# Where the setup's stores of the first m-tile's later queries are issued: from POOL, ahead of the shift rows, to SP, behind the other chunks' keys

## The chip, the cores and the metric

The kernel runs on one core of a Trainium2 chip. The core has a matrix engine (TensorE, PE in the profile), a vector engine (VectorE, DVE), a scalar engine (ScalarE, ACT), GpSimd (POOL) and a sync engine (SyncE, SP) that here only issues DMA transfers. ACT and POOL issue DMA transfers too. The metric is device time in microseconds (us), the median of several executions. Three runs of the kernel before took 1236.10, 1234.47 and 1240.26 us.

## What is computed

Two layers over the same length of 2048 stand side by side, and their outputs are concatenated. Layer A is a long convolution of a state-space model; layer B is attention with 32 query heads of width 18 that share one key and one value head.

```python
def _B_ref(x, wq, wk, wv, wo):
    q = (x @ wq).reshape(B, S, H, Dh).transpose(0, 2, 1, 3)   # S = 2048, H = 32, Dh = 18
    k = x @ wk
    v = x @ wv
    scores = jnp.einsum("bhqd,bkd->bhqk", q, k) * (Dh ** -0.5)
    p = _softmax(scores, axis=-1)
    o = jnp.einsum("bhqk,bkd->bhqd", p, v)
    return o.transpose(0, 2, 1, 3).reshape(B, S, H * Dh) @ wo
```

Layer A forms a kernel K of length 2048 for each of 576 channels out of complex exponentials, convolves it with the input by an FFT of twice the length, and adds the input times a skip weight. The change lies in layer B; layer A fills the engines beside it.

## The kernel before, in words

**Attention.** The 2048 queries are cut into four chunks of 512 (index c), the 576 query columns into m-tiles of seven heads (index m; the last has four). Scores are computed with the keys on the partitions, 128 keys at a time, and 512 queries of one chunk on the free axis, for two heads (a pair) at once. A product in full precision is made of three parts: the operand is rounded (qh, kh), and what rounding leaves (ql, kl) is multiplied separately. So a head's queries stand as 55 rows in an augmented tile (`aug`): rows 0 to 17 hold qh, 18 to 35 qh again, 36 to 53 ql, and row 54 a shift (sh), an upper bound of the scores, which is subtracted before the exponential. Two heads stand at partitions 0 and 64 of one `aug` tile. The keys stand in `kaug` in the matching rows, with ones in row 54.

**The setup** (lines 209 to 304, function `setup`) loads the input and the weights, projects the keys of all four chunks and the queries of chunk 0's first m-tile, and places the keys: `place(c)` issues six transfers of 18 rows on SP (line 281). `place(0)` serves the first scores. Then the first m-tile's queries are made by a generator that `setup` advances, `first_queries` and, in it, `queries(0, 0, ...)`. For the four heads of the first two pairs, `queries` copies the rows straight into the tiles `aug0` and `aug1` (line 363, on POOL, with qh of the second pair on ACT). The other three heads of the m-tile go to DRAM, into `qd` (line 365): one store of qh to rows 0 to 17, one of qh to rows 18 to 35, one of ql, all on POOL. After the shift has been worked out on PE and DVE (aw, up, un, sh), line 387 writes the shift rows of the first two pairs, on ACT and on SP, and line 389 stores the shift of the other three heads to `qd`, on POOL. Then `setup` issues `place(1)` to `place(3)`, and after them the loads of the other m-tiles' weights (line 207), the transform matrices, the convolution's input and the output weights.

**The main loop** (`main`) runs rounds of three scores, each a pair of heads against 128 keys: six matmuls, three exponentials on ACT, and the products with the values (ops). Between them a planner at build time places all other work, the later m-tiles' projections (q), their bounds (up) and the convolution. It uses modelled costs of PE, ACT and DVE and writes out one fixed order for these three engines. The order of SP and of POOL is chosen by the framework, so there an instruction may stand elsewhere than the program's text says. `fetch` (line 398, on SP) reads the 55 rows of later heads from `qd` into the five `aug` tiles, which are used in turn.

**Names that the change touches.** The tiles qh, ql and sh have one buffer each (`bufs=1`): the copies of the second m-tile's queries (DVE, lines 103 and 99, right after the projection q) write to the same memory that the first m-tile's stores read, and wait for them. All projections and bounds share one PSUM bank (`bank`), which is filled again only after DVE has emptied it. Generators yield what they wait for: "v" for vector work, "p" for matrix work, "w" for nothing in particular; a caller's `advance()` runs one on to its next yield.

Of the kernel before, what the change touches and what calls it, by code (L numbers as in the profile page):

```python
# [9 lines left out]
F32 = mybir.dt.float32  # L10
# [11 lines left out]
DH = 18  # L22
# [141 lines left out]
def matmul4(nc, ps, w, x, start=True, stop=True):  # L164

    n = w.shape[-1]
    for j in range(0, n, 32):
        e = min(n, j + 32)
        nc.tensor.matmul(ps[j:e], w[:, j:e], x, start=start, stop=stop, tile_position=(0, j))  # L169


class Attention:
# [36 lines left out]
    def setup(self, tp, conv):  # L209
# [5 lines left out]
        nc, cp, a, V = self.nc, self.cp, self.a, self.V  # L215
# [62 lines left out]
        def place(c):  # L278
            for r, t in ((0, kh), (36, kh), (18, kl)):
                for b in (0, 64):  # L280
                    nc.sync.dma_start(self.kaug[b + r:b + r + 18, c * CT:(c + 1) * CT].bitcast(F32), t[32 * c:32 * c + 18, :].bitcast(F32))
# [10 lines left out]
            side.advance()  # L292
        for c in range(1, NCH):
            place(c)

        for m in range(2, 5):
            V.memset(self.wq[m][0:1, 0, 0:1], 0.0)
# [50 lines left out]
    def queries(self, c, m, qh, ql, ab):  # L348

        nc, V, K = self.nc, self.V, self.k  # L350
        m0, mn = MT[m]
        h0, h1 = m0 // DH, (m0 + mn) // DH
        if m == 0:
            self.qd[c] = self.dr.tile([H, 55, CT], F32, tag="qd", name=f"qd{c}")
        qd = self.qd[c]

        n0 = 4 if (c, m) == (0, 0) else 0
        for h in range(n0):
            t = self.aug[h // 2]
            for row, src in ((0, qh), (18, qh), (36, ql)):  # L360
                b = 64 * (h % 2) + row
                q = nc.scalar if h // 2 == 1 and row < 36 else nc.gpsimd
                q.dma_start(t[b:b + 18, :].bitcast(F32), src[h * DH:h * DH + DH, :].bitcast(F32))
        for row, src in ((0, qh), (18, qh), (36, ql)):
            nc.gpsimd.dma_start(qd[h0 + n0:h1, row:row + 18, :], src[n0 * DH:mn, :].bitcast(F32))  # L365
        self.first = False
        yield "v", 0.0, False
        aw = self.p2.tile([P, P], F32, tag="aw", name=f"aw{c}_{m}", bufs=1)
        V.tensor_scalar(aw[:mn, :], ab[:mn, 0:1].broadcast_to([mn, P]), self.kmax[:mn, 0:1], None, op0=ALU.mult)
        yield "p", max(K.v + 0.4, K.fill), False  # L370

        up = self.bank(8, f"up{c}_{m}")
        matmul4(nc, up, aw[:mn, :], self.sel[:mn, 0:8])
        K.pe(0.1)
        K.v = max(K.v, K.t + 0.3)
        un = self.p2.tile([P, 1], F32, tag="un", name=f"un{c}_{m}", bufs=4)
        V.tensor_reduce(un, up, axis=AX.X, op=ALU.max)
        K.filled()
        if self.ubound is not None:
            u2 = self.p2.tile([P, 1], F32, tag="u2", name=f"u2_{c}_{m}", bufs=4)  # L380
            V.tensor_tensor(u2, un, self.ubound, op=ALU.max)
            un = u2
        self.ubound = un
        sh = self.p2.tile([8, CT], F32R, tag="sh", name=f"sh{c}_{m}", bufs=1)
        V.tensor_scalar(sh, un[0:8, 0:1].broadcast_to([8, CT]), -1.0, None, op0=ALU.mult)
        for pr in range(n0 // 2):
            (nc.scalar, nc.sync)[pr].dma_start(self.aug[pr][54:119:64, :].bitcast(F32), sh[0:2, :].bitcast(F32))
            self.ready.add(pr)
        nc.gpsimd.dma_start(qd[h0 + n0:h1, 54, :], sh[:h1 - h0 - n0, :].bitcast(F32))
        self.queried = c * H + h1  # L390

    def fetch(self, group):
# [922 lines left out]
```

## Time and profile before

| what | us |
|---|---|
| median of three runs | 1236.10 |
| the profiled execution's own time | 1237.14 |
| its span, from the first to the last instruction | 1235.1 |
| PE busy | 1154.1 |
| ACT busy | 1046.1 |
| DVE busy | 987.2 |
| POOL busy | 57.5 |
| first matmul of the setup | 10.08 |
| last matmul of the setup ends | 31.25 |
| first scores of the main loop | 35.67 |

How to read it: the span is that of one profiled execution; its own time is the span and some 2 us around it, and stands 1.0 us above the median. Times in the views count from the span's start. A line gives the engine, the line of the kernel, the operation and the tiles (out<-in); "q" behind an engine's name (SPq, ACTq) marks its queue of DMA issues and register work, where an entry's length is the issue and not the transfer. A bracket at the end gives the idle time ahead of an instruction and what ended it. The granted clock is the share of TensorE's full clock that the chip allowed.

### The profile page before, as it was taken

How to read it: one execution, taken by the hardware profiler on the slowest of the kernel's cores; microseconds unless marked ns; L12 is line 12 of the kernel's file. 1: busy time of each engine (PE TensorE's matmuls, PEld its weight loads, DVE VectorE, ACT ScalarE, POOL GpSimd, SP SyncE). 2: the span in 40 equal slices, each digit the busy share in tenths (PEclk: the TensorE clock that was granted, in tenths of full speed). 3: DMA queues.
4: the chain of work that ended last, by engine and by line, in shares of the span. 5: the costliest groups of instructions: out<-in, count | busy, mean ns of one | idle time of the engine just before them, and what ended most of it. 6: DMA issues, size and time to landing. Idle time of an engine off the chain costs nothing.

```text
span 1235.1 us, 32531 instructions
## 1 busy us (share of the span) xinstructions
PE 1154.1 (93%) x13762; PEld 473.4 (38%) x13762; DVE 987.2 (80%) x1604; ACT 1046.1 (85%) x1101; POOL 57.5 (5%) x97
## 2 busy tenths in 40 slices
PE   5899999999999999999999899999999999899997
PEld 1344334344344344344334334334433334334333
DVE  4668978986987986896898895797798897897753
ACT  2689979989988888888988888888989988999992
POOL 2110000100100000000000000000010000000000
PEclk9899999999999899999999899999999999999999
DMA  7541221222232012023313002122122212012111
GB/s 219 176 133 53 73 69 60 75 75 78 79 104 83 34 38 81 26 72 103 95 57 120 21 20 77 52 76 71 50 75 79 72 35 77 15 51 86 47 41 41
DMA packets 55402, 89.29 MB, mean 72 GB/s; under 512 B 14620, under 2 KB 25244, under 8 KB 54740
## 3 DMA queue, kind: packets, MB, share of 16 engines
q1 hardware_dynamic: 43972, 72.19, 17.9%
q0 software_dynamic: 10592, 14.39, 4.4%
q8 instruction: 110, 1.80, 0.6%
q10 hardware_dynamic: 688, 0.57, 0.2%
q14 instruction: 40, 0.33, 0.1%
HBM read 49.25 MB, written 36.50 MB: 69 GB/s over the span
## 4 chain that ended last, share of the span: by engine, by line
PE 67%; DVE 20%; ACT 6%; issue 4%; DMA 2%; POOL 0%; SPq 0%; ACTq 0%; DVEq 0%
PE ops L708 27%; PE s L409 19%; ACT P L417 5%; PE op L169 4%; DVE tab L99 4%; PE q L169 4%; PE kg L1028 3%; DVE ks L99 3%; PE iy L169 3%; DVE acc L99 2%; DMA xr<-xT 2%; PE hk L169 2%; DVE f L99 1%; DVE r L99 1%; PE lk L169 1%
## 5 line engine op out<-in xcount | busy, mean ns | idle before, releaser
L417 ACT ACTIVATE P<-s 128x1024 f32<-128x1024 f32 x1024 | 967.7, 1030 | 151.2 <-PE s L409 144.1
L708 PE MATMUL ops<-P,v_sb 128*32 128x512 f32 x4096 | 523.4, 603 | 9.9 <-DVE o L103 9.8
L409 PE MATMUL s<-aug,kaug 55*128 55x512 f32 x2048 | 365.4, 444 | 27.3 <-ACT P L417 21.0
L409 PEld LDWEIGHTS s<-aug,kaug 55*128 55x128 f32 x2048 | 170.2, 186 | 344.0 <-ACT P L417 309.6
L708 PEld LDWEIGHTS ops<-P,v_sb 128*32 128x32 f32 x4096 | 115.9, 110 | 160.0 <-issue 120.5
L169 PE MATMUL q<-x,wq_sb 128*32 128x256 f32 (+2 forms) x1480 | 102.7, 396 | 5.1 <-DVE un L111 2.6
L169 PE MATMUL op<-wo_sb,oT 126*32 126x288 f32 (+1 forms) x1088 | 79.7, 416 | 6.2 <-DVE sck L99 3.7
L169 PEld LDWEIGHTS q<-x,wq_sb 128*32 128x32 f32 (+2 forms) x1480 | 46.9, 110 | 57.4 <-issue 27.5
L103 DVE COPY ksb<-kg 128x192 f32<-128x192 f32 x48 | 17.5, 364 | 56.7 <-PE kg L1028 56.7
L99 DVE TENSOR_TENSOR tab<-tab,tt 128x576 f32<-128x576 f32 (+1 forms) x72 | 59.2, 822 | 1.6
L99 DVE TENSOR_TENSOR tab<-tab 128x576 f32<-128x576 f32 (+1 forms) x72 | 59.0, 820 | 0.9
L99 DVE TENSOR_TENSOR tt<-f,sum 128x576 f32<-128x576 f32 (+1 forms) x72 | 58.9, 818 | 0.0
L99 DVE TENSOR_TENSOR tab<-sum,r 128x576 f32<-128x576 f32 (+1 forms) x72 | 58.9, 818 | 0.0
L99 DVE TENSOR_TENSOR tab<-r,dif 128x576 f32<-128x576 f32 (+1 forms) x72 | 58.8, 816 | 0.0
L169 PEld LDWEIGHTS op<-wo_sb,oT 126*32 126x32 f32 (+1 forms) x1088 | 31.9, 111 | 48.3 <-issue 23.9
L365 POOL DMA_DIRECT2D qd<-qh x40 | 25.3, 637 | 514.4 <-DVE qh L103 514.4
L99 DVE TENSOR_TENSOR acc<-acc,pt 128x1728 f32<-128x1728 f32 (+2 forms) x36 | 48.6, 1351 | 0.1
L99 DVE TENSOR_TENSOR pt<-us,ks 128x1728 f32<-128x1728 f32 (+2 forms) x36 | 48.6, 1351 | 0.0
L99 DVE TENSOR_TENSOR sck<-lk,sck 128x384 f32<-128x384 f32 x48 | 24.5, 552 | 29.7 <-PE lk L169 29.7
L1028 PEld LDWEIGHTS kg<-tab 128*32 128x32 f32 x2304 | 36.0, 110 | 23.2 <-issue 9.2
L1028 PE MATMUL kg<-tab 128*32 128x64 f32 x2304 | 41.8, 220 | 1.3 <-DVE tab L99 1.1
L99 DVE TENSOR_TENSOR ks<-ks 128x576 f32<-128x576 f32 (+1 forms) x48 | 41.0, 854 | 0.9
(123 smaller groups left out, 944.5 us busy)
## 6 DMA issues: line engine op xcount, KB each, us to landing
aug<-qd SPq DMA_DIRECT2D x124, 110.0 KB
od<-o SPq DMA_DIRECT2D x31, 256.0 KB
qd<-qh POOLq DMA_DIRECT2D x30, 252.0 KB, 5.2
u<-u SPq DMA_DIRECT2D x12, 384.0 KB
kd<-ksb SPq DMA_DIRECT2D x12, 384.0 KB
kt<-kd SPq DMA_DIRECT2D x48, 96.0 KB
outa<-u SPq DMA_DIRECT2D x12, 384.0 KB
oT<-od SPq DMA_DIRECT2D x16, 252.0 KB
```

The lines of the kernel that those rows point to most:

```text
L99: return self.v.tensor_tensor(out, *a, **k)
L103: return self.v.tensor_copy(out, *a, **k)
L169: nc.tensor.matmul(ps[j:e], w[:, j:e], x, start=start, stop=stop, tile_position=(0, j))
L365: nc.gpsimd.dma_start(qd[h0 + n0:h1, row:row + 18, :], src[n0 * DH:mn, :].bitcast(F32))
L409: nc.tensor.matmul(ps[:, j, :], self.kaug[r, kb * P:(kb + 1) * P], t[r, :], start=True, stop=True)
L417: nc.scalar.activation(pt, ps, AF.Exp, scale=SCALE)
L708: nc.tensor.matmul(o_ps[32 * j:32 * j + 32, :], self.v[:, kb, :], pts[2 * n + j // 2][:, j % 2, :], start=(kb == 0), stop=(kb == 15), tile ...
L1028: nc.tensor.matmul(ps[32 * g:32 * g + 32, d, :], t[:, :32], t[:, 32:], start=(j == 0), stop=(j == 1), tile_position=(0, 32 * g))
```

## The change

The three stores of line 365 become a function `store(q)`, which takes the engine that issues them. For every m-tile but the first of chunk 0 it is called at the old place with POOL. For the first (where four heads went straight into the `aug` tiles, so `n0` is 4) the generator yields once more after the shift rows, and only then issues the three stores and the shift's store, all on SP. In `setup` one `side.advance()` behind the three `place` calls runs this part. So SP issues four more transfers between the last key rows and the weight loads, and POOL four fewer.

```diff
@@ setup
         for c in range(1, NCH):
             place(c)
+        side.advance()
 
         for m in range(2, 5):
@@ queries
-        for row, src in ((0, qh), (18, qh), (36, ql)):
-            nc.gpsimd.dma_start(qd[h0 + n0:h1, row:row + 18, :], src[n0 * DH:mn, :].bitcast(F32))
+        def store(q):
+            for row, src in ((0, qh), (18, qh), (36, ql)):
+                q.dma_start(qd[h0 + n0:h1, row:row + 18, :], src[n0 * DH:mn, :].bitcast(F32))
+        if n0 == 0:
+            store(nc.gpsimd)
         self.first = False
         yield "v", 0.0, False
@@ queries, behind the shift rows
-        nc.gpsimd.dma_start(qd[h0 + n0:h1, 54, :], sh[:h1 - h0 - n0, :].bitcast(F32))
+        q = nc.gpsimd if n0 == 0 else nc.sync
+        if n0:
+            yield "w", 0.0, False
+            store(q)
+        q.dma_start(qd[h0 + n0:h1, 54, :], sh[:h1 - h0 - n0, :].bitcast(F32))
         self.queried = c * H + h1
```

## The prediction

> **What bounds the kernel now.** I read the page first, for the whole span, and the waits of TensorE next.
>
> ```profile
> span 1235.1 us, 32531 instructions
> PE 1154.1 (93%) x13762; PEld 473.4 (38%) x13762; DVE 987.2 (80%) x1604; ACT 1046.1 (85%) x1101; POOL 57.5 (5%) x97
> PE s L409 <- ACT P L417: 21.0, 62, 0.5
> PE s L409 <- DMA qd<-qh: 4.4, 1, 4.4
> ```
>
> PE is busy 93% of the span. Outside the loads at the start its waits are small and many; only one of 4.4 us stands alone, ahead of the first scores. The build writes out one order for PE, ACT and DVE, so a delay of PE early in the main loop can only be made up where PE has slack later. A table of stretches shows how little there is (columns: length, busy time of PE, PEld, DVE, ACT, POOL with instruction counts, granted clock, DMA share, GB/s).
>
> ```profile
> 31.25:35.67 4.42, 0.00 (x0) 0.03 (x1) 4.25 (x12) 0.00 (x0) 1.11 (x2) 0.85 0.40 97
> 35.67:41.20 5.53, 5.53 (x42) 2.93 (x46) 3.41 (x8) 2.86 (x3) 0.00 (x0) 0.50 0.22 63
> 41.20:48.68 7.48, 7.48 (x83) 3.05 (x75) 3.63 (x7) 6.19 (x7) 1.86 (x3) 1.00 0.42 115
> 48.68:61.00 12.32, 12.32 (x148) 4.95 (x146) 9.42 (x14) 10.89 (x12) 0.55 (x1) 1.00 0.87 290
> 200.00:1190.00 990.00, 942.19 (x11304) 388.29 (x11298) 826.36 (x1322) 876.12 (x921) 35.74 (x57) 0.99 0.20 64
> ```
>
> PE is full from 35.67 to 61 and 95% busy (942.19 of 990) in the long middle. So whatever shift PE has when it comes out of the first 60 us, I carry to the end one for one. The second row matters too: after 4.42 us without a matmul PE works for 5.53 us at a granted clock of 0.50, which costs half of that, 2.8 us.
>
> What holds the first scores? They read the augmented queries and the keys, and nothing of qd, so the name in the wait is not the cause. The timeline of ACT, SP and POOL and the table of DMA issues (last number: us from issue to landing) show what is under way:
>
> ```profile
> 29.84 0.61 ACTq L387 DMA_DIRECT2D aug<-sh  x1
> 30.77 0.57 SPq L387 DMA_DIRECT2D aug<-sh  x1
> 31.38 13.95 SPq L281 DMA_DIRECT2D kaug<-keys  x17
> ...
> 27.93 2.01 POOL L363 DMA_DIRECT2D aug<-ql  x4
> 29.92 1.31 POOL L365 DMA_DIRECT2D qd<-qh  x2
> 31.22 0.61 POOL L365 DMA_DIRECT2D qd<-ql  x1
> 31.82 0.54 POOL L389 DMA_DIRECT2D qd<-sh  x1
> ...
> aug<-ql POOLq DMA_DIRECT2D x4, 36.0 KB, 2.6
> qd<-qh POOLq DMA_DIRECT2D x2, 108.0 KB, 5.9
> qd<-ql POOLq DMA_DIRECT2D x1, 108.0 KB, 5.8
> qd<-sh POOLq DMA_DIRECT2D x1, 6.0 KB, 5.6
> ```
>
> The two shift rows are the last writes that the first scores need. They go out at 29.84 and 30.77, PE starts at 35.67, so they took up to 5.8 and 4.9 us, while the queries' rows just before landed in 2.6. In between stand POOL's stores; even the one of 6 KB needed 5.6. The stores delay the shift rows: this is what the change takes out.
>
> **The change, part by part.** *The shift rows.* Without the stores I give them the 2.6 us of the ql rows: 30.77 + 2.6 = 33.4, so PE would start at about 33.4, 2.3 us earlier (bounds: nothing, and 4.4, all of its idle time). POOL loses four issues, 2.5 us of an engine that is 5% busy: nothing.
>
> *The stores on SP.* They now stand behind seventeen key rows. The rows of line 281:
>
> ```profile
> 32.20 13.13 SPq L281 DMA_DIRECT2D kaug<-keys  x16
> L281 SPq DMA_DIRECT2D kaug<-keys x24: 697/698/2001, 24.8 to 44.6; - x24
> 45.44 0.88 SPq L207 DMA_DIRECT2D wq_sb<-wq  x2
> ```
>
> One of the sixteen took 2.00 us, while POOL's stores ran; the other fifteen take (13.13 - 2.00)/15 = 0.742 each. With all at that pace the keys end at 31.38 + 17 x 0.742 = 44.0 (45.3 if the long one stays). SP's issues of such rows cost 0.74 with the gap, so the stores go out at 44.0, 44.7 (qh), 45.5 (ql), 46.2 (shift row), and the next loads at about 46.9 in place of 45.44.
>
> *A new wait on DVE.* The tiles qh, ql and sh have one buffer each. The second m-tile's queries overwrite qh and ql, so their DVE copies must wait until the stores have read the first ones. Before, the stores had landed by 31.22 + 5.8 = 37.0 and the copy came at 44.94, waiting only for PE. Rows of DVE, then of PE:
>
> ```profile
> 44.94 0.69 DVE L103 CAST qh<-q 126x512 fp32r<-126x512 f32 x1 [5.86 <-PE q L169]
> 45.67 0.69 DVE L99 TENSOR_TENSOR ql<-q,qh 126x512 fp32r<-126x512 f32 x1
> 46.99 0.29 DVE L107 TENSOR_SCALAR aw<-ab,kmax 126x128 f32<-126x128 f32 x1
> 49.33 0.16 DVE L111 TENSOR_REDUCE un<-up 128x1 f32<-128x8 f32 x1
> ...
> 47.55 1.20 PE L409 MATMUL s<-aug,kaug 55*128 55x512 f32 x6
> 48.68 0.25 PE L169 MATMUL up<-sel_sb,aw 126*32 126x8 f32 x8
> 51.49 1.93 PE L169 MATMUL q<-x,wq_sb 128*32 128x256 f32 x32
> ```
>
> No store of this kind runs on SP before. Its landing time is bounded below by the 36 KB rows' 2.6 us and above by the worst store row (8.7 us, below); I take 5.8, the ql store of the same shape. Then qh is free at 44.7 + 5.9 = 50.6 and ql at 45.5 + 5.8 = 51.3. From the start of the ql subtraction to the end of aw DVE needs 47.28 - 45.67 = 1.6, so aw ends at 52.9 and up can run at 53.0, against 48.68: **4.3 us later**. With the bounds 2.6 and 8.7 it is 48.1 + 1.7 = 49.8 (1.1 later) and 54.2 + 1.7 = 55.9 (7.2 later).
>
> Who waits behind: on DVE the table products of the convolution from 47.20 on, then un and sh; on PE, in its fixed order, behind up stand products with the values, the next scores and the third m-tile's projection; ACT gets no scores meanwhile. The 2.3 us won at the start go into this wait: PE, earlier by 2.3, comes to up at about 46.4 and stands there 6.6 us. What DVE owes afterwards is covered: it sits idle 4.31 us before the next qh (row below), and PE's q at 51.49 came 2.0 us after un (49.33 + 0.16) and keeps that distance.
>
> *The clock.* A PE that stands for 6.6 us is the case of the table's first two rows. I charge 2.5 us for the half clock after it (bounds 0, and the 2.8 of the old stage). The half clock that PE has now at 35.67 may go, but that too lies ahead of up and is lost in the wait.
>
> *What moves on SP.* Every later load slips by about 1.5 us, more where stores and loads share the engines.
>
> ```profile
> 62.62 0.69 DVE L103 CAST qh<-q 126x512 fp32r<-126x512 f32 x1 [4.31 <-PE q L169]
> 60.00 5.67 SPq L398 DMA_DIRECT2D aug<-qd  x6
> 70.26 1.36 PE L409 MATMUL s<-aug,kaug 55*128 55x512 f32 x6
> qd<-qh POOLq DMA_DIRECT2D x2, 252.0 KB, 6.2
> qd<-ql POOLq DMA_DIRECT2D x1, 252.0 KB, 8.7
> SPq L1049 <- DMA kd<-ksb: 37.0, 12, 5.1
> ```
>
> The fetch of the next pairs, issued from 60.00 to 65.67, is first read by the eleventh group of scores at 70.26: 4.6 us of cover, and 11 with PE's own shift. It costs nothing; uncovered it would cost PE a microsecond for each one of slip. The second m-tile's stores, some 6 us later on POOL, have until the DVE copy at 62.62 plus the shift, against landings of 6.2 and 8.7 us from 45.93 on: covered as well.
>
> *The sum.* 4.3 + 2.5 = 6.8 us. The profiled execution took 1237.1 us (span 1235.1 and 2.0 around it), 1.0 above the median of the runs; so it would take 1243.9, and the median 1236.1 + 6.8 = **1242.9**.
>
> [...]
>
> **The rivals.** *Stores that queue up behind each other.* If the three serve one after another, the ql store lands like the later one of the second tile: 8.7 us where qh took 6.2 (rows above). Then up comes at 55.9: 7.2 + 2.5 = 9.7, **1245.8**. For it: in that row the last of three is the late one. Against it: POOL's first three landed in 5.9 and 5.8. [...]
>
> *Stores that land fast.* The 384 KB store kd on SP made its reader wait 37.0/12 = 3.1 us on average; with that, ql is free at 48.6, up comes at 50.3, 1.6 late; with 2.6 us it is 1.1. Add 1.7 to 2.5 for a shorter half clock: about **1239.5**. For it: SP is otherwise quiet at 44 us, POOL was not at 30. Against: the shape is POOL's, and 6 KB there took 5.6.
>
> *No new wait, the gain kept.* If the copy of the second qh did not find the stores in its way, or they landed by 44, PE keeps 2.3 us and perhaps 2.8 of the half clock: **1231 to 1234**, not slower. It decides only if ql is free by about 44.7 (PE at up at 46.4 less 1.7), before the ql store is even issued at 45.5; so it needs another order of SP than the one named.
>
> *Late queries for the second group.* If SP's slip exceeds some 11 us, the scores at 70.26 wait for the fetch: at the point where it decides, 1243 and up, **1250** with 7 us past it. Against: 1.5 us of slip in issues, and 330 KB of stores beside loads that run at 290 GB/s, about 1 us.
>
> That SP does not put the stores there at all (its order is not written out by hand) would leave 1236.
>
> **How the numbers follow.** Forecast 47% (own range 1239.8 to 1244.4, from landings of 3.5 to 7 us and 1.7 to 2.8 for the clock); queued stores 20%; fast landing 17%; gain kept 9%; late fetch 4%; no effect 3%. The range 1234.5 to 1249.5 leaves out the larger part of the kept gain below and of the late fetch above, and holds both bounds of the landing time. A measurement of this kernel tells about 0.5%, 6.2 us, from no change: the line is at 1242.3. Of the forecast's 47 some 28 lie above it, with 20 of the queued stores and 4 of the late fetch: slower 0.52. Faster by 6.2 takes more than all that is to be won at the start, 0.03. The rest, 0.45, is within.
>
> **What would show it.** After: the wait for the first scores shrinks from 4.4 to about 2; SP issues stores at 44 to 46; DVE's qh copy, which waited for PE, is released by a DMA at about 50.6, with some 7 us or more of idle time; PE stands before up until about 53, and the granted clock is 0.50 behind it. Were up at 47 or earlier, the new wait is not there and the gain stands; were the clock full behind the wait, 2.5 us come off; were PE's shift at 61 us not the difference at the end, the carrying one for one is wrong.

## The result, and the profile after

| kernel | runs | median us | lowest to highest |
|---|---|---|---|
| before | 6 | 1238.85 | 1234.47 to 1241.27 |
| changed | 6 | 1248.20 | 1243.97 to 1248.97 |

The changed kernel is slower: ratio 1.0070, 95% interval 1.0052 to 1.0089, which is 8.7 us (6.4 to 11.0); the two medians themselves lie 9.35 us apart. Its profiled execution took 1245.1 us, 8.0 above the profiled one of before and 3.1 below the median of its own runs.

The page of the changed kernel, its first line, the busy times, and three rows of its waits (us in total, times, longest):

```profile
span 1243.0 us, 32528 instructions
PE 1154.1 (93%) x13762; PEld 472.7 (38%) x13762; DVE 987.6 (79%) x1604; ACT 1045.7 (84%) x1101; POOL 55.1 (4%) x93
...
PE up L169 <- DVE aw L107: 9.1, 1, 9.1
PE s L417 <- DMA aug<-sh: 1.6, 1, 1.6
DVE ql L99 <- DMA qd<-ql: 1.4, 1, 1.4
```

PE's busy time is what it was, 1154.1; the 7.9 us that the span is longer are idle time. The wait of 4.4 us for the first scores is down to 1.6, and one of 9.1 us, which was not there, stands ahead of up.

The timelines of SP, PE and DVE show how the two hang together (start, length, then the idle time ahead and what ended it):

```profile
29.62 0.56 SPq L391 DMA_DIRECT2D aug<-sh  x1
30.23 12.65 SPq L281 DMA_DIRECT2D kaug<-keys  x17
42.98 1.46 SPq L367 DMA_DIRECT2D qd<-qh  x2
44.48 0.66 SPq L367 DMA_DIRECT2D qd<-ql  x1
45.19 0.55 SPq L397 DMA_DIRECT2D qd<-sh  x1
45.85 2.38 SPq L207 DMA_DIRECT2D wq_sb<-wq  x3
```

```profile
31.90 1.92 PE L417 MATMUL s<-aug,kaug 55*128 55x512 f32 x6 [1.59 <-DMA aug<-sh]
...
42.92 1.19 PE L417 MATMUL s<-aug,kaug 55*128 55x512 f32 x6
53.24 0.29 PE L169 MATMUL up<-sel_sb,aw 126*32 126x8 f32 x8 [9.13 <-DVE aw L107]
53.37 3.27 PE L716 MATMUL ops<-P,v_sb 128*32 128x512 f32 x16
56.57 0.96 PE L417 MATMUL s<-aug,kaug 55*128 55x512 f32 x6
57.47 1.93 PE L169 MATMUL q<-x,wq_sb 128*32 128x256 f32 x32
```

```profile
49.49 0.69 DVE L103 CAST qh<-q 126x512 fp32r<-126x512 f32 x1 [11.34 <-DMA wq_sb<-wq]
51.57 0.69 DVE L99 TENSOR_TENSOR ql<-q,qh 126x512 fp32r<-126x512 f32 x1 [1.39 <-DMA qd<-ql]
52.89 0.30 DVE L107 TENSOR_SCALAR aw<-ab,kmax 126x128 f32<-126x128 f32 x1
```

The first scores begin 2.3 us after the shift row's issue at 29.62 (before: 4.9). The stores go out behind seventeen key rows, at 42.98 to 45.19. The second m-tile's queries are ready by 40.2, but DVE's copy into qh comes at 49.49, the subtraction into ql at 51.57, aw at 52.89, up at 53.24. The copy's row names a load of weights as the releaser; the copy reads nothing of it. What it overwrites is what the store of qh reads, and the next row names the store of ql rightly; the experiments below separate the two. The second store of qh was issued at 43.7, the copy ran 5.8 us later; the ql store was issued at 44.48, the subtraction ran 7.1 us later.

Behind the wait the granted clock is low, 0.51. The stretches of the changed kernel (columns as in the prediction's table):

```profile
43.50:53.24 9.74, 0.61 (x4) 0.19 (x2) 2.33 (x5) 2.88 (x4) 1.93 (x3) 0.62 0.65 207
53.24:56.20 2.96, 2.96 (x24) 0.70 (x24) 2.86 (x7) 0.00 (x0) 0.00 (x0) 0.51 1.00 294
56.20:61.00 4.80, 4.80 (x56) 2.14 (x52) 4.73 (x6) 3.07 (x4) 0.54 (x1) 1.00 0.96 344
```

Sixteen products with the values take 3.27 us at 53.37 where they took 1.90 before. At the third m-tile's projection PE is 57.47 - 51.49 = 5.98 us late. How that is carried on is seen in the copies of finished groups, 31 over the whole kernel (count, shortest/median/longest in ns, first and last start); the row of before, then that of the changed kernel:

```profile
L103 DVE COPY o<-ops x31: 671/685/693, 78.5 to 1184.1; 128x512 f32<-128x512 f32 x31
```

```profile
L103 DVE COPY o<-ops x31: 671/683/693, 84.5 to 1192.2; 128x512 f32<-128x512 f32 x31
```

The first comes 6.0 us later than before, the last 8.1.

### The profile page after: what moved, and what is told of

The parts are those of the page before. It is cut to its first block, busy times and chain, and to the rows that moved or that the text cites. A ratio compares the mean times of both kernels' runs of the same rounds, so it can differ in the third digit from the quotient of the medians.

```text
span 1243.0 us, 32528 instructions
## 1 busy us (share of the span) xinstructions
PE 1154.1 (93%) x13762; PEld 472.7 (38%) x13762; DVE 987.6 (79%) x1604; ACT 1045.7 (84%) x1101; POOL 55.1 (4%) x93
## 4 chain that ended last, share of the span: by engine, by line
PE 62%; DVE 24%; ACT 6%; issue 4%; DMA 4%; ACTq 0%; SPq 0%; DVEq 0%
PE ops L716 25%; PE s L417 18%; ACT P L425 5%; DVE tab L99 4%; PE op L169 4%; DVE ks L99 3%; PE q L169 3%; PE kg L1036 3%; PE iy L169 3%; DVE acc L99 2%; DVE r L99 2%; DVE f L99 2%; DMA xr<-xT 2%; PE hk L169 2%; DVE pt L99 1%
```

## The experiments

The theory that I held first was the prediction's: the copies of the second m-tile wait for the stores, because the tiles have one buffer and the stores go out late and land slowly. The rivals were that the stores' place on SP delays later loads, and that the low clock or the transfers of the stores cost the time in another way. The first four kernels ran on one chip beside 35 runs of before (median 1240.16), the next four beside 29 (1239.37), the last beside 13 (1239.81).

**The wait taken away, the stores left where they are.** qh, ql and sh of the first m-tile live in three `aug` tiles that are not used yet, so nothing has to wait for their stores.

```diff
@@ operands
+        if (c, m) == (0, 0):
+            return self.ring[3], self.ring[4], self.p2.tile([P, 2], F32, tag="ab", name=f"ab{c}_{m}")
@@ queries
-        sh = self.p2.tile([8, CT], F32R, tag="sh", name=f"sh{c}_{m}", bufs=1)
+        sh = self.ring[2][:8, :] if n0 else self.p2.tile([8, CT], F32R, tag="sh", name=f"sh{c}_{m}", bufs=1)
```

> The changed kernel, but the first m-tile's qh, ql and sh lie in the augmented tiles 2 to 4, which stand empty until about 60 us, so that the second m-tile's copies overwrite nothing the stores still read. The stores stay on SP behind the keys. Theory (the loss is the DVE wait for the stores and the half clock behind it): DVE's second qh copy is released by PE again, at about 41, TensorE stands before up for under 0.5 us, and the 3.7 us stay that the changed kernel is ahead at its first scores and the projection behind them: 3 to 4 us less than the kernel before, ratio about 0.997. Rival (the loss is the slip of SP's later loads, or the stores' traffic beside them): the wait before up goes, but TensorE waits somewhere else before 80 us and the time stays at 4 us over the kernel before or more.

Measured: ratio 1.0053 (1.0035 to 1.0071). The forecast of 0.997 was missed. DVE's wait was gone, its copy ran at 42.29, released by PE, and up followed at 46.04 without a wait. But PE then stood as long at the next place. Its timeline there, and SP's:

```profile
58.08 3.64 PE L169 MATMUL q<-x,wq_sb 128*32 128x256 f32 x32 [9.16 <-DMA wq_sb<-wq]
```

```profile
45.34 2.85 SPq L369 DMA_DIRECT2D qd<-aug  x3
48.24 2.32 SPq L399 DMA_DIRECT2D qd<-aug  x1
50.66 2.50 SPq L207 DMA_DIRECT2D wq_sb<-wq  x3
```

The third m-tile's weights (wq_sb, line 207) stand on SP behind the stores and reach PE only at 58.08, 7.4 us after their issue. Before, PE took them at 51.49 without a wait. So the slip of SP's later loads, which the prediction had put at nothing, is a second wait beside the first: in the changed kernel DVE's wait hides it, since PE comes to the weights only at 57.47. Its size here, 9.16 us, is in part this kernel's own: the four issues of the stores took 5.2 us on SP (45.34 to 50.56) where they took 2.8 in the changed kernel (42.98 to 45.74). The second m-tile's stores, which DVE's copy no longer holds back, went out on POOL beside them (43.28 to 45.21); that they are what lengthened SP's issues was not tried.

**The form of the store.** The three stores write to a buffer of their own, 54 rows in one piece each, in place of three heads of 18 rows in `qd`; each of these heads is then fetched in four transfers in place of one.

```diff
@@ queries
+        if n0:
+            self.q3 = self.dr.tile([3, 54, CT], F32, tag="q3", name="q3")
...
-            for row, src in ((0, qh), (18, qh), (36, ql)):
-                q.dma_start(qd[h0 + n0:h1, row:row + 18, :], src[n0 * DH:mn, :].bitcast(F32))
+            for j, (row, src) in enumerate(((0, qh), (18, qh), (36, ql))):
+                dst = self.q3[j] if n0 else qd[h0:h1, row:row + 18, :]
+                q.dma_start(dst, src[n0 * DH:mn, :].bitcast(F32))
```

> The changed kernel, with the three stores going to a buffer of their own in which the 54 rows of one store lie one behind the other, in place of three heads with a gap between; the same bytes, engine, place and order. Twelve short fetches read them back in place of three, from 60 us on. In the changed kernel DVE's ql waits until 51.57 for a ql store issued at 44.48, 7.1 us. [...] If it is the loads beside it or the writing to DRAM itself, ql stays at 51 or later and the time at 7 us over or more.

Measured: 1.0014 (0.9994 to 1.0034). Its SP, DVE and PE:

```profile
43.55 0.79 SPq L372 DMA_DIRECT2D q<-qh  x2
44.39 0.32 SPq L372 DMA_DIRECT2D q<-ql  x1
```

```profile
46.56 0.69 DVE L103 CAST qh<-q 126x512 fp32r<-126x512 f32 x1 [7.84 <-DMA q<-qh]
47.28 0.69 DVE L99 TENSOR_TENSOR ql<-q,qh 126x512 fp32r<-126x512 f32 x1
```

```profile
48.96 0.25 PE L169 MATMUL up<-sel_sb,aw 126*32 126x8 f32 x8 [3.10 <-DVE aw L107]
```

At the same place on SP the same 108 KB were read 2.5 us after the issue (44.03 to 46.56) where the three-head form took 5.8, and ql was free 2.9 us after its issue at the latest, where it took 7.1. The wait ahead of up fell from 9.13 to 3.10 us. So the landing time is a matter of the form, and the wait is one for the stores, not for weights, which are issued here too, at 45.22. No view shows which DMA engines carried a store, and no other form was tried, so why the form matters is not shown.

**The place of the stores.** Two kernels move the whole step ahead on SP: one to behind the second chunk's keys, one to before all of them (there the framework put one of the qh stores even ahead of the second shift row).

```diff
@@ setup, behind the second chunk's keys
-        for c in range(1, NCH):
-            place(c)
-        side.advance()
+        place(1)
+        side.advance()
+        for c in range(2, NCH):
+            place(c)
@@ setup, ahead of all
+        side.advance()
         for c in range(1, NCH):
             place(c)
-        side.advance()
```

> The changed kernel with the stores on SP behind the first of the three other chunks' keys, that is 12 key rows earlier, all behind the shift rows. Theory: the ql store is issued 12 x 0.742 = 8.9 us earlier, at 35.6, and lands at about 42.6; DVE waits for it by a microsecond at most, which TensorE covers with the products and scores ahead of up; first scores as in the changed kernel: 3 to 4 us under the kernel before, the same as with the tiles of their own. Rival (slip of SP's loads): the same slip as in the changed kernel, so a time of 4 us over the kernel before or more.

> The changed kernel with the stores on SP ahead of all keys of the other chunks (18 rows' issues later in turn). One of the qh stores comes out ahead of the second shift row in SP's order. Theory: the ql store is issued at about 32 and lands by 39, before DVE's copy of the second qh at 41, so there is no wait on DVE; the shift row of the second pair is held up by the one store ahead of it, so the first scores gain less than in the changed kernel, 1 to 2.5 us; time 1 to 3 us under the kernel before. Rival (SP is the wrong queue for these stores wherever they stand, because key rows or loads behind them come late): scores wait for keys near 41 us, and the time is no less than before.

Measured: 1.0023 (1.0005 to 1.0042) and 1.0031 (1.0010 to 1.0052). The first of them, DVE, PE and SP:

```profile
42.54 0.69 DVE L99 TENSOR_TENSOR ql<-q,qh 126x512 fp32r<-126x512 f32 x1 [0.57 <-DMA qd<-ql]
```

```profile
52.22 3.64 PE L169 MATMUL q<-x,wq_sb 128*32 128x256 f32 x32 [4.33 <-DMA wq_sb<-wq]
```

```profile
35.09 1.45 SPq L368 DMA_DIRECT2D qd<-qh  x2
36.59 0.66 SPq L368 DMA_DIRECT2D qd<-ql  x1
...
37.90 10.57 SPq L281 DMA_DIRECT2D kaug<-keys  x12
48.58 1.61 SPq L207 DMA_DIRECT2D wq_sb<-wq  x3
```

Both forecasts, of less time than before, were missed. Both lost DVE's wait and gained another one for the same weights, 4.33 and 5.06 us, with slow matmuls behind it: 3.64 us for the projection's 32, against 1.93. The theory was widened: two waits side by side, and each place of the stores ahead of the weights on SP meets one of them.

**The weights moved too.** Four kernels tell the two waits apart. In each the third m-tile's weights go out ahead of the third and fourth chunks' keys: with the stores behind the second chunk's keys; with the stores as in the change; with the tiles of their own and the stores as in the change; and in the kernel before.

```diff
@@ setup (with the stores as in the change)
-        for c in range(1, NCH):
+        place(1)
+        weights(2)
+        for c in range(2, NCH):
             place(c)
         side.advance()
-        for m in range(2, 5):
+        for m in range(3, 5):
-            V.memset(self.wq[m][0:1, 0, 0:1], 0.0)
-            self.load_wq(m)
+            weights(m)
```

`weights(m)` holds the two removed lines. In the first of the four `side.advance()` stands between `place(1)` and `weights(2)`.

> The stores are issued behind the second chunk's keys alone, and the third m-tile's weights right behind the stores, ahead of the other two chunks' keys. Theory now held, two waits side by side: with the stores at this place alone the DVE's wait was gone (0.57 us left) and PE stood 4.33 us for the third m-tile's weights, issued at 48.6 us; issued at about 38.5 us they land before 46, some 2 us before PE asks, so neither wait is left, PE keeps the 2.7 us that its first scores come earlier, and without a stall no half clock follows it: 3 us or so under before, ratio 0.9965 to 0.999. Rival, the weights are late because the stores' packets hold the queues, wherever they are issued: PE still stands 2 to 4 us for them, ratio 1.001 to 1.003 as with the stores moved alone. Rival, what is won at 50 us is given back later by half-clock stretches that the new pace brings: no wait before 60 us, a shift of about -3 us at 73 us, and 0 or more at the end.

> The changed kernel with one load moved: the third m-tile's weights go out on SP ahead of the third and fourth chunks' keys; the stores stay behind all keys. Theory now held: the DVE's copies still wait for the stores, which go out at about 45 us (1.5 us of weights more ahead of them), so up comes at 53 to 54 us, the weights never end a wait, and the time is as the changed kernel's, ratio 1.005 to 1.009. Rival, the weights alone cost the time in the changed kernel: 0.998 to 1.002.

> The changed kernel, the stores where the change puts them, with both waits taken away: the first m-tile's qh, ql and shift row in tiles of their own (alone it gave 1.0053, PE standing 9.16 us for the third m-tile's weights issued at 50.7 us) and those weights ahead of the third and fourth chunks' keys. Theory now held: up comes with no wait at about 45 us, the third m-tile's queries with none at about 49, and the 2 to 3 us that the first scores come earlier stay: ratio 0.9965 to 0.999. Rival, the place of the stores costs by itself, through later loads on SP or their packets: a third wait shows behind these two, and the ratio stays at 1.002 or above.

> The kernel before with one load moved, the third m-tile's weights ahead of the third and fourth chunks' keys. Theory now held: in before PE does not stand for these weights, so nothing is won or lost: ratio 0.9985 to 1.0015, and first scores as in before, near 35.7 us. Rival, the weights bound before as well, or an earlier load delays the keys: outside those bounds.

| kernel | ratio | PE stands before up | for the weights | for the first fetch | first group copy against before | last |
|---|---|---|---|---|---|---|
| changed | 1.0070 (1.0052 to 1.0089) | 9.13 | no | no | +6.0 | +8.1 |
| own tiles | 1.0053 (1.0035 to 1.0071) | no | 9.16 | no | +8.7 | +11.0 |
| weights early, stores as changed | 1.0082 (1.0051 to 1.0112) | 9.53 | no | no | +7.1 | +9.5 |
| stores behind one chunk's keys | 1.0023 (1.0005 to 1.0042) | no | 4.33 | no | +3.1 | +5.6 |
| the same, weights early | 0.9993 (0.9976 to 1.0009) | no | no | no | -2.6 | -0.9 |
| own tiles, weights early | 1.0003 (0.9983 to 1.0022) | no | no | 4.23 | +1.8 | +2.4 |
| before, weights early | 1.0002 (0.9986 to 1.0018) | no | no | no | -0.3 | +0.2 |

With only the weights moved, the wait for the stores and the cost stay as in the changed kernel; in before the same move does nothing. So the weights are not what the changed kernel pays for. With both waits taken away the cost is gone, from 1.0070 to 1.0003, though the stores stand where the change put them. Here the rival was half right: a third wait showed, but the ratio did not stay at 1.002. PE, then SP of the kernel with own tiles and early weights:

```profile
70.27 1.13 PE L423 MATMUL s<-aug,kaug 55*128 55x512 f32 x2 [4.23 <-DMA aug<-qd]
```

```profile
55.37 4.53 SPq L314 DMA_DIRECT2D wo_sb<-wo  x5
60.55 7.27 SPq L412 DMA_DIRECT2D aug<-qd  x6
```

PE was 4.9 us ahead of before at the third m-tile's projection (46.59 against 51.49), which is more than the cover of 4.6 us that the prediction gave this fetch. The kernel with the stores behind one chunk's keys was 2.6 ahead and met no wait. My forecast of 0.9965 to 0.999 for both was missed. For this last kernel its second rival fits, that what is won early is given back later: 2.6 us ahead at the first group copy, 0.9 at the last, and nothing won that the interval shows.

**A third load moved.** In the kernel with own tiles and early weights the five loads of the output weights are issued behind the first fetch.

```diff
@@ main
-        self.load_wo()
@@ fetch
             self.next += 1
+            if self.next == 5:
+                self.load_wo()
```

> The kernel with tiles of their own and the third m-tile's weights early, and also the five loads of the output weights (4.53 us on SP from 55.37 us there) issued behind the first fetch of the next pairs, which went out at 60.55 us while PE stood 4.23 us for it. Theory, a third wait in the same row, SP's order: the fetch goes out at 54 to 56 us and lands before PE asks at 66; no wait, no half clock behind it (6.8 us of it there), so the 4.9 us that it was ahead of before at 48 us are still there at 110 us; at the end 2 to 5 us under before, since half-clock stretches later take up to 2 us: ratio 0.996 to 0.9985. Rival, the stores' or the second m-tile's stores' landing holds the fetch, not SP's order: PE still stands 3 to 4 us at 66 and the ratio stays at 1.000. Rival, a lead this early is given back later whatever its size: no wait at 66, but 0.9985 to 1.001.

Measured: 1235.91 us against 1239.81, ratio 0.9969 (0.9956 to 0.9981): faster than both kernels. SP, and PE's scores that had stood for the fetch:

```profile
57.22 5.93 SPq L412 DMA_DIRECT2D aug<-qd  x6
63.85 4.41 SPq L314 DMA_DIRECT2D wo_sb<-wo  x5
```

```profile
67.56 1.36 PE L425 MATMUL s<-aug,kaug 55*128 55x512 f32 x6
```

The fetch goes out 3.3 us earlier and the wait is gone. Half of the expectation failed: the lead was 2.7 us and not 4.9 (up at 45.97 against 43.77), because this execution had the low clock at 35 us (granted 0.77 from 30 to 45 us, against 1.00 in the kernel with own tiles and early weights), in the first projection (4.42 us for 40 matmuls against 2.37). At a lead of 2.7 the old fetch might have done as well, so that this move is what brings the gain is not shown; that PE meets no further wait between the first scores and 75 us is. The kernel with the stores behind one chunk's keys and early weights points the same way: it met no wait either and was 2.6 us ahead at the first group copy, where this one was 2.7, yet it measured 0.9993 (0.9976 to 1.0009). And in this profiled execution, the slowest of the nine, the last group copy comes 1.1 us later than in before. Why the one kernel is faster over its runs and the other is not stays open.

## Why the prediction was right, and where it was not

**The sign and the mechanism were right.** Slower, through a new wait of DVE's copies for the stores, PE standing before up, low clock (0.51) behind it. The forecast was 6.8 us at 61 us of the span; the trace shows 5.98. The time at the end is 8.7 us, 1.9 more than forecast, and the median lies 5.3 above the predicted 1242.9, of which 2.75 is the median of before, which came out at 1238.85 with more runs; the rest is what the two medians' difference of 9.35 has over the 6.8.

*The shift rows.* Taken at 2.6 us, they allowed PE to start 2.3 us after the issue at 29.62. The setup was 0.9 us earlier in this execution (up to the transposed values, line 304: 29.65 against 30.59), so of the 3.8 us by which the first scores came earlier 2.8 are left for the change, where 2.3 was forecast. But this pair of executions makes it look larger than it may be. The kernel before with early weights issues the same up to here, POOL's stores included, and its PE stood half as long:

```profile
34.64 2.54 PE L413 MATMUL s<-aug,kaug 55*128 55x512 f32 x6 [2.22 <-DMA qd<-qh]
```

Reckoned from the same point of the setup (31.77 there), the gain against that execution is 0.6. In the eight kernels whose stores stand on SP behind the shift rows this wait was 1.4 to 1.8 us, so the change does shorten it; by how much hangs on the execution of the old order, whose wait was 4.43 us once and 2.22 the other time.

*The stores on SP.* Seventeen rows at 12.65/17 = 0.744 us, as forecast (0.742); the long row of 2.00 us is gone. The stores went out 1.0 earlier than the 44.0 of the prediction, only because SP began 1.15 earlier.

*The new wait.* Here one term was off: qh needed the 5.8 us that were taken, ql 7.1 in place of 5.8. The two are freed 2.1 us apart although they were issued 0.8 apart, which fits the rival of stores that queue behind each other, in part. The early SP and the late ql cancel: up at 53.24, forecast 53.0. That the two times agree is luck. Against the setup of this execution it is 5.5 late rather than 4.3.

*The clock.* Charged 2.5, measured 3.27 - 1.90 = 1.4: the low clock began while PE stood (granted 0.98 from 44.20 to 46.00, 0.50 from there to 53.24) and lasted only 2.96 us past up (0.51, then 1.00).

*What moves on SP "costs nothing".* This was the step that failed, without a cost in the changed kernel. It named the fetch and the second m-tile's stores, and left out the third m-tile's weights, the first load behind the stores. Had DVE not had to wait, PE would have come to these weights at about 46.9 (the scores ahead of up end at 44.1, and from up to there PE took 2.8 in before), 1 us after their issue at 45.85, and would have stood for them, as it did in the kernel with own tiles. So the rival "the gain kept", 1231 to 1234, was priced too low: with the copies' wait gone the kernel took 6.6 us more than before (1.0053). The rival of stores that land fast, 3.4 over before, left the weights out too, but they did not bind there: in the other form of the store, with ql free 2.9 us after its issue at the latest, PE met no wait for them and the kernel took 1.7 us more than before (1.0014).

*One for one to the end.* On the mean it held, for this pair of executions not: the shift is 6.0 us at the first group copy and 8.1 at the last, which is the sign that the prediction had set for this step being wrong. The three rows of windows from before and the changed kernel show why (granted clock is the third number from the right):

```profile
340.00:345.00 5.00, 4.00 (x22) 1.39 (x26) 5.00 (x8) 3.59 (x5) 0.00 (x0) 0.66 0.49 152
630.00:645.00 15.00, 13.00 (x100) 4.20 (x96) 14.46 (x19) 10.59 (x12) 1.86 (x3) 0.89 0.32 96
1070.00:1082.00 12.00, 12.00 (x138) 4.92 (x130) 11.79 (x18) 10.47 (x12) 0.00 (x0) 1.00 0.09 26
```

```profile
340.00:345.00 5.00, 4.95 (x52) 1.67 (x48) 4.93 (x7) 4.80 (x6) 1.11 (x2) 1.00 0.14 45
630.00:645.00 15.00, 13.00 (x141) 5.01 (x136) 14.89 (x17) 12.20 (x13) 1.85 (x3) 1.00 0.14 38
1070.00:1082.00 12.00, 8.86 (x108) 4.24 (x108) 8.49 (x14) 9.24 (x9) 0.00 (x0) 0.86 0.01 3
```

Before has low clock in the first two (0.66 and 0.89 against 1.00), the changed kernel in the third (0.86 against 1.00). Between the group copies around the first two the shift falls by 0.9 us each time (7.03 to 6.15, 6.61 to 5.71), around the third it rises by 0.7 (6.48 to 7.18); from the first group copy to the last it lies between 4.9 and 8.2. Over the seven kernels of the table the measured difference (ratio less one, times the median of before) and the shift at the first group copy are 8.7 and 6.0, 6.6 and 8.7, 10.2 and 7.1, 2.9 and 3.1, -0.9 and -2.6, 0.4 and 1.8, 0.2 and -0.3: apart by 3.1 at most, in both directions, and by 0.6 on the mean. The three kernels outside the table have 1.7 and 2.2 (the other form), 3.8 and 4.6 (ahead of all keys), -3.8 and -2.7 (the third load moved).

## What to carry to other kernels

A store moved behind other work on a queue held its source tile longer here (DVE's copy into it came at 49.49 where it had come at 44.94): look for the next writer of that tile, and for the first load behind the store, and price both, since here the one wait hid the other, which was 9.16 us once the first was gone. When one wait is taken away, work out what is late next before crediting the gain; here there were three in a row. One kernel without any of them was measurably faster (0.9969), another, as far ahead at the first group copy, was not (0.9993), so that a wait is gone does not yet say that its time is won. Where a store must be quick, its form is worth a look: three heads of 18 rows held their source for 5.8 to 7.1 us, 54 rows in one piece for 2.5 to 2.9.

## What was not expected of the hardware

The same gap of PE gave low clock in one execution and not in the other. PE's timeline of before, and then of the changed kernel, at two waits for a group's copy:

```profile
341.00 1.43 PE L708 MATMUL ops<-P,v_sb 128*32 128x512 f32 x8 [1.64 <-DVE o L103]
637.96 1.44 PE L708 MATMUL ops<-P,v_sb 128*32 128x512 f32 x8 [1.95 <-DVE o L103]
```

```profile
348.03 1.07 PE L716 MATMUL ops<-P,v_sb 128*32 128x512 f32 x8 [1.66 <-DVE o L103]
644.58 1.07 PE L716 MATMUL ops<-P,v_sb 128*32 128x512 f32 x8 [1.95 <-DVE o L103]
```

Gaps of 1.6 and 1.95 us stand in both, and the eight products behind them take 1.43 and 1.44 us in one and 1.07 in the other. The granted clock over these products was 0.70 in before, both times, and 0.50 in the stretch behind them (342.43 to 345.00 and 639.40 to 640.90); in the changed kernel it was 1.00 over them and behind them (to 352.00 and 648.00). What brought the low clock stays open.
